# Casting transfers for queries and keys, and three score tiles a batch on VectorE, in a fused attention and soft mixture-of-experts kernel

## The chip, the cores and the metric

One core of a Trainium2 chip. The metric is the device time of one launch in microseconds (us). Every kernel was timed several times beside the kernel before on the same chip. A run can fall in a slower state, here counted from 1.5% above the fastest run of the same kernel.

## The reference, cut to what matters

```python
# q, k, v: 8 batches x 12 heads x 448 x 64, float32; cap = 30
scores = np.matmul(q, k.transpose(0, 1, 3, 2)) / np.sqrt(64)
scores = cap * np.tanh(scores / cap)
attn = softmax(scores)                       # over the keys
x = np.matmul(attn, v)                       # -> 3584 x 768
logits = x @ phi                             # 768 x 32
slot_in = softmax(logits, axis=0).T @ x      # over all 3584 rows
# ... 8 small expert networks on slot_in ...
out = softmax(logits, axis=1) @ slot_out
```

The tanh and the exponential of all scores, 96 heads x 448 x 448 each, are what ScalarE has to do.

## The kernel before: the parts that matter

A *quad* is four heads, a *batch* three quads. The main loop runs 56 iterations j; seven make a batch, and m stands for j mod 7. An iteration has slots a, b, c and d, in which side jobs are issued, so the order of each engine's queue is fixed by the program. The code below is shortened; cuts are marked by dots. Each iteration handles six score tiles of 128x448.

```python
psT = pool("psT", bufs=1, space=PSUM)     # tag "T": one bank for all small transposes and sums
psV = pool("psV", bufs=1, space=PSUM)     # tag "pv": one bank for the value products
...
    def cast(nm, Q):                       # float32 -> bf16 on VectorE, then transposes of 128x128
        t = cst.tile([P, NT, P], BF16, ...)
        dve.tensor_copy(t.rearrange(...), raws.pop((nm, Q)).rearrange(...))
        casts[nm, Q] = t
        if Q > 1:
            load(nm, Q + 1)
...
    shared = [j for j in range(NCH - 2) if j % 7 == 3 and j > 7] if cap < 80 else []
    def poly_exp(j, part):                 # exp of one tile on VectorE, in three parts
        if part == 0:   ...                # three tensor_scalar
        elif part == 1: ...                # two scalar_tensor_tensor
        else:           ...                # two more
...
    def e_norm(b):                         # sum of exp(logits): zps in bank "T", then zacc
        ps = psT.tile([P, 1], F32, name="zps", tag="T")
        ...
            dve.tensor_tensor(zacc, ps, zacc, op=ALU.add)
...
    def spare(n):                          # n filler matmuls into bank "pv"
        busy(n, psV.tile([P, 2, VW], F32, name="junk", tag="pv")[:, 0, 0:P])
...
    for j in range(NCH):                   # one iteration, shortened
        run(j, "0")
        tanh_chunk(2 * j); tanh_chunk(2 * j + 1); exp_chunk(j - 1)   # ScalarE
        pv_pass(pr, 0)                     # TensorE pv; VectorE rec, xq
        run(j, "a")
        qk_chunk(2 * j + 2)                # TensorE scores
        run(j, "b")
        pv_pass(pr, 1)
        run(j, "c")
        qk_chunk(2 * j + 3)
        run(j, "d")
```

The softmax here doesn't subtract the row's maximum and nothing guards it: scores larger than these inputs give would overflow.

## Time and profile before

| | |
|---|---|
| time | 317.54 us median of 3 (317.26 to 317.74) |
| ScalarE | busy 281.3 us, 89% of the span |
| TensorE | busy 269.4 us, 86% |
| VectorE | busy 193.7 us, 62% |
| one batch, from the first scores at m = 4 to the same of the next batch | 32.68 us, five times running |

The chain that ended last is ScalarE for two thirds, and TensorE's waits inside the loop are short. These are the chain by engine ("issue" is time in which an engine waited for nothing that the profile shows), then two rows of the list of waits (who waited for whom: total us, times, longest). In the rows, sc are the scores, kps and qps the transposes of keys and queries, zps and zacc the column sum and its total, pv the value products, rec and xq their scaling, xp, xm and xe tiles of the polynomial, vbd the values that GpSimd casts, and junk the fillers.

```profile
ACT 67%; PE 20%; DVE 5%; issue 3%; DMA 2%; DVEq 0%; ACTq 0%
```

```profile
PE sc L269 <- ACT ex L278: 7.9, 19, 0.7
PE kps L237 <- DVE zacc L383: 1.2, 5, 0.2
```

The scores wait for ScalarE to free their buffer (7.9 us), so TensorE has a little slack. The key transposes wait for zacc for 0.2 us at a time.

### The profile page before, as it was taken

To read this page: it belongs to the slowest core of one execution; us is meant where nothing else is said; L and a number is where in the kernel's file an instruction comes from. 1 tells how busy PE (TensorE), PEld (TensorE's weight loads), DVE (VectorE), ACT (ScalarE), POOL (GpSimd) and SP (SyncE) were. 2 spreads that over 40 slices of the span, in tenths; PEclk is the share of its full clock that TensorE was granted. 3 is DMA by queue.
4 is the path that set the end of the run, shared out by engine and by line. 5 is a ranking of instruction groups with operands and counts; after the bars stand their busy time and mean duration, and the time that the engine had idled before them with its cause. 6 is when DMAs were issued, how large, how long until landed. Compare 5 with 4: busy or idle time off the path is not lost.

```text
span 314.8 us, 8844 instructions
## 1 busy us (share of the span) xinstructions
PE 269.4 (86%) x3804; PEld 191.0 (61%) x3804; DVE 193.7 (62%) x473; ACT 281.3 (89%) x208; POOL 106.5 (34%) x134
## 2 busy tenths in 40 slices
PE   7899898899889998898889989898889998998720
PEld 6667665667666665666666666666666677743400
DVE  3636565766586659575867587657766574327840
ACT  4999999999999999999999999999999999326730
POOL 2464342523543452354245416441732130200000
PEclk9999999999999999999999999999999999999985
DMA  8899999799999999999999999999999807898997
GB/s 223 267 234 238 291 244 269 159 231 256 235 210 231 266 237 207 254 220 266 194 225 269 221 264 190 242 235 266 209 232 254 214 14 207 290 393 301 389 411 314
DMA packets 57479, 77.68 MB, mean 247 GB/s; under 512 B 3809, under 2 KB 53601, under 8 KB 57441
## 3 DMA queue, kind: packets, MB, share of 16 engines
q0 software_dynamic: 30480, 25.22, 52.1%
q1 hardware_dynamic: 26672, 51.68, 48.1%
q8 instruction: 29, 0.48, 0.6%
q10 hardware_dynamic: 288, 0.23, 0.2%
q14 instruction: 10, 0.07, 0.1%
HBM read 91.32 MB, written 18.87 MB: 350 GB/s over the span
## 4 chain that ended last, share of the span: by engine, by line
ACT 67%; PE 20%; DVE 5%; issue 3%; DMA 2%; DVEq 0%; ACTq 0%
ACT ex L278 33%; ACT ex L282 32%; PE pv L318 5%; PE sc L269 3%; PE so_ps L676 2%; PE junk L506 2%; PE hp L649 2%; ACT ob L754 1%; PE op L702 1%; DMA kraw<-in_k_dram 1%; DVE xq L329 1%; PE op L745 1%; PE xps L344 1%; DMA out_dram<-obh 1%; DVE ob L752 1%
## 5 line engine op out<-in xcount | busy, mean ns | idle before, releaser
L278 ACT ACTIVATE ex<-sc 128x1344 bf16<-128x1344 f32 (+1 forms) x113 | 162.3, 1693 | 0.9 <-PE sc L269 0.8
L282 ACT ACTIVATE ex<-ex 128x2688 bf16<-128x2688 bf16 (+4 forms) x58 | 159.2, 2779 | 0.1
L318 PEld LDWEIGHTS <-ex 128*128 128x128 bf16 x1344 | 78.7, 97 | 21.5 <-DVE xq L329 17.8
L318 PE MATMUL pv<-vbd,ex 128*128 128x130 bf16 x1274 | 88.6, 220 | 2.6 <-ACT ex L282 0.7
L269 PE MATMUL sc<-qT,kT 64*64 64x448 bf16 x672 | 78.6, 358 | 8.2 <-ACT ex L278 7.9
L247 POOL CAST vbd<-vraw 64x896 bf16<-64x896 f32 x23 | 21.5, 936 | 103.6 <-PE pv L318 65.3
L269 PEld LDWEIGHTS <-kT 64*64 64x64 bf16 x672 | 27.3, 105 | 25.3 <-issue 7.5
L329 DVE TENSOR_TENSOR xq<-pv,rec 128x256 bf16<-128x256 f32 x91 | 38.6, 424 | 3.1
L328 DVE RECIPROCAL rec<-pv 128x4 f32<-128x4 f32 x91 | 16.5, 181 | 32.1 <-PE pv L318 31.2
L506 PEld LDWEIGHTS <-ones 128*128 128x128 bf16 x470 | 28.6, 100 | 11.6 <-DVE xq L329 8.0
L372 POOL COPY e<-E 128x512 bf16<-128x512 bf16 x9 | 7.2, 795 | 81.5 <-ACT E L366 49.6
L506 PE MATMUL junk<-ones 128*128 128x128 bf16 x433 | 31.4, 219 | 2.5 <-DVE xq L329 1.6
L239 DVE COPY kT<-kps 128x896 bf16<-128x896 bf16 x23 | 14.4, 625 | 24.6 <-PE kps L237 24.4
L109 POOL DMA_DIRECT2D w1b<-in_moe_w_dram x32 | 25.2, 791 | 0.0
L248 POOL CAST vbd<-vraw 64x896 bf16<-64x896 f32 x23 | 23.7, 1029 | 1.3
L346 DVE COPY xT<-xps 128x512 bf16<-128x512 bf16 x47 | 19.5, 415 | 3.2 <-PE xps L344 3.0
L344 PE MATMUL xps<-ident,xq 128*128 128x128 bf16 x188 | 18.1, 218 | 0.2 <-DVE zacc L383 0.2
L239 DVE COPY qT<-qps 128x896 bf16<-128x896 bf16 x23 | 14.2, 616 | 5.2 <-PE qps L237 5.2
L226 DVE CAST kbf<-kraw 128x896 bf16<-128x896 f32 x22 | 16.0, 728 | 1.3 <-DMA kraw<-in_k_dram 1.3
L237 PE MATMUL kps<-ident,kbf 128*128 128x128 bf16 x161 | 12.8, 219 | 4.2 <-DVE slacc L418 2.2
L237 PE MATMUL qps<-ident,qbf 128*128 128x128 bf16 x161 | 12.8, 219 | 3.2 <-DVE lg L360 2.7
L237 PEld LDWEIGHTS <-kbf 128*128 128x128 bf16 x161 | 10.0, 97 | 9.0 <-issue 8.3
(113 smaller groups left out, 255.5 us busy)
## 6 DMA issues: line engine op xcount, KB each, us to landing
w1b<-in_moe_w_dram POOLq DMA_DIRECT2D x32, 384.0 KB, 10.2
vraw<-in_v_dram SPq DMA_DIRECT2D x23, 448.0 KB, 6.6
qraw<-in_q_dram SPq DMA_DIRECT2D x22, 448.0 KB, 7.8
kraw<-in_k_dram SPq DMA_DIRECT2D x22, 448.0 KB, 6.0
w2d<-in_moe_w_dram POOLq DMA_DIRECT2D x20, 384.0 KB, 9.2
w2t<-w2d SPq DMA_DIRECT2D x20, 384.0 KB, 5.9
out_dram<-ob SPq DMA_DIRECT2D x8, 768.0 KB, 7.3
w2b<-in_moe_w_dram POOLq DMA_DIRECT2D x12, 384.0 KB, 9.9
```

Source lines behind the costliest of these rows:

```text
L109: pool.dma_start(out=w1b[e][:, js, fs], in_=w1r[:, e, js, fs])
L237: pe.transpose(ps[:, c, :], src[:, c, :], ident)
L239: dve.tensor_copy(t, ps)
L247: pool.tensor_copy(t[0:HP, :, :, 0:DH], raw[0:HP])
L248: pool.tensor_copy(t[HP:P, :, :, DH + 1:VW - 1], raw[HP:P])
L269: pe.matmul(sc[cs, u, 0:S], qkT["k", Q][r, c, cs], qkT["q", Q][r, :, cs], start=True, stop=True)
L278: act.activation(exs[j][:, half * CS + u0:half * CS + u1, :], sc[:, u0:u1, 0:S], ACT.Tanh, scale=qk_scale / cap)
L282: act.activation(exs[j][:, u0:u1, :], exs[j][:, u0:u1, :], ACT.Exp, scale=cap)
L318: pe.matmul(pvs[pr, half][:, n, 0:VW], exs[j][:, u, GOFF[g]:GOFF[g] + P], vbds[Q % 2][:, h, c, :], start=(c == 0 and n == 0), stop=(c == N ...
L329: dve.tensor_tensor(xq[Q][:, 2 * half:2 * half + 2, h * P:(h + 1) * P] .rearrange("p g (i d) -> p g i d", i=2), pv[:, :, :, 0:DH], rec.to_ ...
L344: pe.transpose(ps[:, g, :], xq[Q][:, g, h * P:(h + 1) * P], ident)
L506: pe.matmul(junk if home is None else home, ones, ones, start=True, stop=True)
```

## The change

Its intent is to relieve ScalarE: two more tiles a batch (m = 1 and m = 6 beside m = 3) get their exponential on VectorE. To make room there, VectorE's casts of queries and keys are dropped for all but the first two quads; the transfers cast on the way, issued by GpSimd. The keys then lie by heads, and fourteen transposes of half width take the place of seven.

```diff
     def load(nm, Q):
-            sp.dma_start(out=t, in_=quad_ap(nm, Q))
+            (sp if nm == "v" else pool).dma_start(out=t, in_=quad_ap(nm, Q))   # bf16 tile for q, k
...
     def transp(nm, Q):
         for c in range(NT):
-            pe.transpose(ps[:, c, :], src[:, c, :], ident)
+            if Q == 1: ...
+            for h in range(2):
+                pe.transpose(ps[h * HP:h * HP + HP, c, :], src[:, h, c * DH:(c + 1) * DH], ident)
...
-    shared = [j for j in range(NCH - 2) if j % 7 == 3 and j > 7] if cap < 80 else []
+    shared = [j for j in range(NCH - 2) if j % 7 in (1, 3, 6) and j > 7] if cap < 80 else []
...
-        at(j + 2, "d" if b == 0 else "a", spare, 4 if b == 0 else 14)
+        at(j + 2, "d" if b == 0 else "a", spare, 4 if b == 0 else 12)
...
     for j in shared:
-        for dj, slot, part in ((0, "a", 0), (0, "c", 1), (0, "d", 2)):
-            at(j + dj, slot, poly_exp, j, part)
+        for slot, part in (("a", 0), ("c", 1)):
+            at(j, slot, poly_exp, j, part)
+        at(*((j, "d") if j % 7 == 3 else (j + 1, "b")), poly_exp, j, 2)
```

Cut: the special path of the first two quads, whose tiles move to a borrowed weight buffer, and the removal of the cast jobs; in their slots the loads are issued now.

## The prediction

> **What bounds the kernel now.** I read the page, then the chain of waits in order of time, then the groups by shape, then one stretch of the timeline. Line numbers are those of the kernel before.
>
> ```profile
> PE 269.4 (86%) x3804; PEld 191.0 (61%) x3804; DVE 193.7 (62%) x473; ACT 281.3 (89%) x208; POOL 106.5 (34%) x134
> ```
>
> The reader is to see that ScalarE and TensorE are both close to full over the span, VectorE far from it.
>
> ```profile
> 56.91 2.36 ACT ex L278 x2
> 59.27 1.96 ACT ex L282
> 61.23 2.36 ACT ex L278 x2
> 63.59 2.33 ACT ex L282
> ```
>
> That is the chain: tanh of two chunks (2.36 us), then exp of one group of six score tiles (2.33 us), without a gap, from about 20 us to 216 us. Where VectorE takes one tile the exp is 1.96 us. So a tile is worth 0.37 us of ScalarE. (The recorded busy time of one tanh grows along the trace while the ends stay 1.18 us apart; I use ends.) A batch is seven loop iterations; I write m for the iteration modulo 7. A batch takes 14 x 1.18 + 6 x 2.33 + 1.96 + 0.20 = 32.7 us.
>
> TensorE is close behind. In most batches it waits for ScalarE to free a score buffer in only three iterations, m = 2, 3, 4:
>
> ```profile
> 183.96 0.75 PE L269 MATMUL sc<-qT,kT 64*64 64x448 bf16 x6 [0.22 <-ACT ex L278]
> ...
> 188.86 0.76 PE L269 MATMUL sc<-qT,kT 64*64 64x448 bf16 x6 [0.52 <-ACT ex L278]
> ...
> 211.95 0.76 PE L269 MATMUL sc<-qT,kT 64*64 64x448 bf16 x6 [0.49 <-ACT ex L278]
> ```
>
> 0.22 + 0.52 + 0.49 = 1.2 us of slack in a batch of 32.7. Its scores finish 1.2 to 2.9 us before ScalarE wants them. The rest of its idle time is waiting for VectorE, one round trip after another, because one PSUM bank serves all small transposes and sums ("T") and one serves the value products ("pv"):
>
> ```profile
> 199.46 0.41 DVE L346 COPY xT<-xps 128x512 bf16<-128x512 bf16 x1
> ...
> 199.79 0.61 DVE L226 CAST kbf<-kraw 128x896 bf16<-128x896 f32 x1
> ...
> 200.72 0.18 DVE L328 RECIPROCAL rec<-pv 128x4 f32<-128x4 f32 x1 [0.31 <-PE pv L318]
> ...
> 200.93 0.42 DVE L329 TENSOR_TENSOR xq<-pv,rec 128x256 bf16<-128x256 f32 x1
> ...
> 201.58 0.16 DVE L383 TENSOR_TENSOR zacc<-zps,zacc 128x1 f32<-128x1 f32 x1 [0.23 <-PE zps L379]
> ...
> 201.79 0.55 PE L237 MATMUL kps<-ident,kbf 128*128 128x128 bf16 x7 [0.25 <-DVE zacc L383]
> ```
>
> Here (m = 6) the key transposes wait until VectorE has read the tiny sum out of their bank. The order of VectorE's queue therefore sets TensorE's pace, however low its share is.
>
> ```profile
> 204.07 0.62 DVE L226 CAST qbf<-qraw 128x896 bf16<-128x896 f32 x1
> ...
> 204.90 0.18 DVE L328 RECIPROCAL rec<-pv 128x4 f32<-128x4 f32 x1 [0.21 <-PE pv L318]
> ...
> 205.46 0.61 DVE L239 COPY qT<-qps 128x896 bf16<-128x896 bf16 x1
> ...
> 206.12 0.35 PE L355 MATMUL lps<-phib,xT 128*128 128x32 bf16 x8
> ```
>
> At m = 0 the logits wait for qT in the same way.
>
> [...] the weight casts are all issued by POOL, 0.78 us each. [...] six score matmuls of 448 columns take 0.57 to 0.76 us, seven full-width transposes of 128 columns 0.56 us. [...] 382 to 394 ns for the polynomial's tensor_scalar steps, 613 to 872 ns for its two-tensor steps on the same 448 elements.
>
> **The change part by part.**
>
> ScalarE: shared groups go from 7 to 20 (m = 1, 3, 6 with j from 8 to 53). 13 x 0.37 = 4.8 us less. A batch falls to 31.9 us. Alone this would give 317.5 - 4.8 = 312.7 us.
>
> VectorE: it loses two casts in each of 22 quads: 22 x (0.728 + 0.660) = 30.5 us. It gains 13 polynomials. One is 0.382 + 0.394 + 0.394 (part 0), 0.613 + 0.626 (part 1), 0.666 + 0.872 (part 2) = 3.95 us; 13 x 3.95 = 51.4 us. Net +20.9 us, 194 to 215 us, still under 70%. As starts in the queue the parts occupy about 1.23, 1.31 and 1.50 us.
>
> TensorE: 44 transposes of seven become fourteen of half width, 308 more matmuls. The two heads write different column halves, so I expect pairs to overlap and the path to grow by only some 0.03 us a call. Two fillers fewer per batch give back about 0.1 us.
>
> GpSimd and the transfers: 44 more issues x 0.78 = 34 us on an engine busy 34% and mostly waiting. The loads are issued a whole quad ahead, with two buffers, and bytes read stay the same; the tightest needs its keys some 2.7 iterations (12 us) after the issue, against a median landing of 10 us for the larger weight pieces. I take these as hidden.
>
> **The path through TensorE and VectorE**, placing the new parts where the emitted order has them, starting from the shown stretch:
> - m = 6: part 0 stands behind xT: 199.87 + 1.23 = 201.1, so rec is 0.4 late, xq ends at 201.7. Part 1 stands before zacc: 201.7 + 1.3 = 203.0, zacc to 203.15, key transposes at 203.2 in place of 201.79: +1.4 us. The cast removed there blocked nothing, since rec was waiting for TensorE.
> - m = 0: shifted by 1.4, xT ends at 205.6. Part 2 follows: 207.1, then rec, in place of 204.90: +2.2. qT and the logits follow: about 208.35 for 206.12, +2.2.
> - m = 1 and 2: part 0 delays the second rec by another 0.5; the fillers wait for it (+2.75). The 0.5 us that TensorE used to wait for ScalarE is used up (+2.15). Then part 2 stands between kT and the logits' addition: 0.65 later, the query transposes wait for their bank: +2.8 at the products of m = 3.
> - m = 3, 4: from the first rec of m = 3 to the products of m = 4 VectorE is continuous already (183.79 to 189.71), unchanged: still +2.8. At m = 4 and 5 nothing is added, and the casts removed there stood beside waits.
>
> So this loop takes about 32.7 + 2.8 = 35.5 us a batch, against ScalarE's 31.9: VectorE's queue and TensorE's waits become the bound, and ScalarE starves by 3.6 us a batch. There are six such passes (j = 13 to 53): 16.8 us, plus about 0.5 for j = 8. TensorE's lead over ScalarE at the end, about 2.5 us, is lost once in return: 317.5 + 17.3 - 2.5 = 332 us. I shade this to 330, as part of VectorE's work may slide into gaps that I took as shut.
>
> **The rivals.**
> - ScalarE stays the bound: 312 to 316 us. For it: the chain is ScalarE for 65% of the span, and VectorE would still be idle over 30%. Against it: only 1.2 us of TensorE slack a batch, of which ScalarE's gain alone takes 0.75.
> - About half of the added VectorE work is hidden: the loop stays near 32 to 33.5 us, 314 to 322 us, within 2%.
> - The half-width transposes do not pair: 7 x 0.056 = 0.39 us a call, six calls a batch, +2.3 us a batch on the loop, total about 345. Against it: the score matmuls pair in this trace.
> - The keys arrive late, behind weight pieces in one queue: several us of TensorE waiting for transfers. Against it: ordering ahead of time; I give it little.
>
> **Range and chances.** The hand-walked loop is my main case, 62%, from 324 to 339. Half-hidden or bound by ScalarE within 2%: 30%. The full 4.8 us is only 1.5%, so faster by over 2% needs a second gain (shorter VectorE queue without the casts); 8%. The range 312 to 339 holds both main cases.
>
> **What would show it.** Right: in the changed profile ScalarE has gaps before tanh released by TensorE's scores, a few us a batch; the key transposes at m = 6 wait over 1 us for zacc; the logits' addition and rec wait behind polynomial steps; batches are about 35 us apart. Wrong: tanh and exp stay back to back with batches of 31.9 us (then VectorE's order did not matter), or TensorE waits for transfers, or seven pairs of transposes take 0.8 us.

## The result, and the profile after

The changed kernel takes 337.63 us (median of 4, 337.00 to 338.95); the kernel before took 317.64 us beside it. The ratio is 1.062 (95% interval 1.056 to 1.068): 6% slower. Ratios here are the mean time of one kernel's fast runs over that of the other's in the same rounds, so not quite the ratio of the medians quoted.

The page of the changed kernel, its engines, its chain and the granted TensorE clock in 40 slices (in tenths):

```profile
PE 279.3 (83%) x4098; PEld 196.8 (58%) x4098; DVE 217.1 (64%) x520; ACT 279.7 (83%) x208; POOL 140.3 (42%) x178
...
PEclk9999999978999799979999999989999999999995
...
PE 42%; DVE 36%; ACT 14%; DMA 3%; issue 2%; DVEq 0%; ACTq 0%
```

The chain has passed from ScalarE to TensorE and VectorE taking turns, though VectorE is busy only 64% of the time. The clock row, which before was 9 everywhere but in the last two slices, has dips. Rows of the list of waits:

```profile
ACT ex L286 <- PE pv L326: 16.2, 9, 3.2
PE kps L245 <- DVE zacc L391: 10.8, 5, 2.2
ACT ex L286 <- PE sc L277: 6.2, 13, 1.2
```

ScalarE now starves for 22 us behind TensorE, and the wait for zacc is 2.2 us where it was 0.2. One such place, m = 6, in the timeline (start, duration, engine, line, operation, out<-in, count, and in brackets the idle time before and what ended it):

```profile
215.59 1.07 POOL L255 CAST vbd<-vraw 64x896 bf16<-64x896 f32 x1 [4.50 <-PE pv L326]
...
216.14 0.25 PE L387 MATMUL zps<-ones,e 128*128 128x1 bf16 x4
216.34 0.80 DVE L308 SCALAR_TENSOR_TENSOR xp<-xm 128x448 f32<-128x448 f32 x1
216.70 1.25 POOL L256 CAST vbd<-vraw 64x896 bf16<-64x896 f32 x1
217.17 1.25 DVE L309 SCALAR_TENSOR_TENSOR xp<-xp,xm 128x448 f32<-128x448 f32 x1
218.35 0.14 DVE L391 TENSOR_TENSOR zacc<-zps,zacc 128x1 f32<-128x1 f32 x1
218.55 0.63 PE L245 MATMUL kps<-ident,kb 128*64 128x128 bf16 x14 [2.16 <-DVE zacc L391]
219.11 1.70 PE L326 MATMUL pv<-vbd,ex 128*128 128x130 bf16 x14
...
222.62 1.29 ACT L286 ACTIVATE ex<-sc 128x1344 bf16<-128x1344 f32 x1 [3.02 <-PE pv L326]
```

Three things are to be seen. The sum of one column, 0.14 us of work, stands behind part 1 of the polynomial. Part 1 itself took 0.80 + 1.25 us, while GpSimd cast v beside it; without a cast beside it the same two operations take 0.61 and 0.62 us (the second 0.91 in three of seven places). The second cast too was longer, 1.25 us where its median in the kernel before is 0.96. And after the wait the pv products took 1.70 us; elsewhere they take 0.98. Windows around two such places, without and with the dip (us, busy and count of PE, PEld, DVE, ACT, POOL, then the granted clock, DMA share, GB/s):

```profile
178.00:182.00 4.00, 2.94 (x39) 1.88 (x37) 3.53 (x10) 4.00 (x3) 1.81 (x2) 1.00 1.30 205
182.00:186.00 4.00, 2.89 (x50) 2.27 (x50) 3.01 (x7) 2.38 (x3) 4.00 (x6) 1.00 0.79 171
...
216.00:220.00 4.00, 1.84 (x31) 1.58 (x28) 3.08 (x5) 3.60 (x3) 3.96 (x5) 0.87 1.18 179
220.00:224.00 4.00, 4.00 (x50) 2.75 (x49) 2.86 (x8) 1.29 (x1) 0.82 (x2) 0.70 1.18 240
```

The clock was granted by half from 218.9 on for 3.41 us. The trace's clock records show this four times in the loop: at 72.2 (for 6.83 us), 109.7, 147.3 and 218.9 (3.41 us each), 17.07 us in all; before there is none before the tail. The records hold two values only, 1.0 and 0.5. The starts lie 37.55, 37.55 and 71.68 us apart, which is 11, 11 and 21 times 3.413, and the stretches are 1 or 2 times 3.413 us long. So the clock changed on a grid of 3.413 us here (an estimate from these starts and lengths). The identical wait at 181 us (2.16 us of TensorE idle, as at 216 us) drew no half clock, and its place in the grid tells the two apart. In the three traces with this wait (changed, f2_v_later, f3_m3_m6) there are 18 of them. With grid lines every 3.413 us from the first start of half clock, the 13 that began 0.0 to 2.2 us after a line were followed by half clock at the next, the 5 that began 2.9 to 3.0 us after one were not. No run moved the grid on purpose. TensorE's busy share of one step of the grid does not decide: in the changed kernel the step from 68.77 us was 64% busy and the clock was lost behind it, that from 181.40 us was 50% busy and the clock was kept. What does decide was not shown.

Where the 22.4 us between the two profiled spans (314.8 and 337.2 us) arose: the six batches from the scores at m = 4 of j = 11 to those of j = 53 took 218.61 us for 196.65, so +21.96; the rest is -0.55 ahead of them and about +1 behind. These are the scores at both ends, first before, then after:

```profile
58.14 0.76 PE L269 MATMUL sc<-qT,kT 64*64 64x448 bf16 x6 [0.52 <-ACT ex L278]
...
254.79 0.76 PE L269 MATMUL sc<-qT,kT 64*64 64x448 bf16 x6
```

```profile
57.59 0.76 PE L277 MATMUL sc<-qT,kT 64*64 64x448 bf16 x6
...
276.20 0.76 PE L277 MATMUL sc<-qT,kT 64*64 64x448 bf16 x6
```

### The profile page after: what moved, and what is told of

Its sections match the earlier page's. It is cut to its first block, busy times and chain, and to the rows that moved or that the text cites. A ratio compares the mean times of both kernels' runs of the same rounds, so it can differ in the third digit from the quotient of the medians.

```text
span 337.2 us, 9443 instructions
## 1 busy us (share of the span) xinstructions
PE 279.3 (83%) x4098; PEld 196.8 (58%) x4098; DVE 217.1 (64%) x520; ACT 279.7 (83%) x208; POOL 140.3 (42%) x178
## 4 chain that ended last, share of the span: by engine, by line
PE 42%; DVE 36%; ACT 14%; DMA 3%; issue 2%; DVEq 0%; ACTq 0%
PE pv L326 15%; DVE xq L337 7%; ACT ex L286 7%; ACT ex L290 6%; PE sc L277 6%; DVE xp L309 4%; PE junk L515 4%; PE kps L245 4%; DVE ex L312 3%; DVE xp L311 3%; DVE rec L336 3%; DVE xm L304 2%; DVE xp L308 2%; DVE xe L306 2%; DVE qT L247 2%
## 5 line engine op out<-in xcount | busy, mean ns | idle before, releaser
L286 ACT ACTIVATE ex<-sc 128x1344 bf16<-128x1344 f32 (+1 forms) x113 | 141.2, 1305 | 22.9 <-PE pv L326 16.2
L290 ACT ACTIVATE ex<-ex 128x2688 bf16<-128x2688 bf16 (+4 forms) x58 | 131.3, 2268 | 0.1
L326 PEld LDWEIGHTS <-ex 128*128 128x128 bf16 x1344 | 81.2, 100 | 28.4 <-DVE xq L337 20.5
L326 PE MATMUL pv<-vbd,ex 128*128 128x130 bf16 x1274 | 92.7, 225 | 5.8 <-DVE xq L337 4.1
L255 POOL CAST vbd<-vraw 64x896 bf16<-64x896 f32 x23 | 23.4, 1017 | 101.5 <-PE pv L326 92.0
L277 PEld LDWEIGHTS <-kT 64*64 64x64 bf16 x672 | 25.7, 106 | 20.0 <-issue 2.3
L245 PE MATMUL kps<-ident,kb 128*64 128x128 bf16 x308 | 13.7, 230 | 15.8 <-DVE zacc L391 10.8
L256 POOL CAST vbd<-vraw 64x896 bf16<-64x896 f32 x23 | 25.7, 1118 | 1.3
L245 PEld LDWEIGHTS <-kb 128*64 128x64 bf16 x308 | 11.6, 114 | 19.1 <-issue 18.8
L309 DVE SCALAR_TENSOR_TENSOR xp<-xp,xm 128x448 f32<-128x448 f32 x20 | 21.6, 1078 | 0.7
L167 POOL DMA_DIRECT2D qb<-in_q_dram x22 | 16.1, 734 | 3.2 <-DVE kT L206 3.2
```

The lines of the kernel that those rows point to most:

```text
L245: pe.transpose(ps[h * HP:h * HP + HP, c, :], src[:, h, c * DH:(c + 1) * DH], ident)
L256: pool.tensor_copy(t[HP:P, :, :, DH + 1:VW - 1], raw[HP:P])
L277: pe.matmul(sc[cs, u, 0:S], qkT["k", Q][r, c, cs], qkT["q", Q][r, :, cs], start=True, stop=True)
L286: act.activation(exs[j][:, half * CS + u0:half * CS + u1, :], sc[:, u0:u1, 0:S], ACT.Tanh, scale=qk_scale / cap)
L290: act.activation(exs[j][:, u0:u1, :], exs[j][:, u0:u1, :], ACT.Exp, scale=cap)
L309: dve.scalar_tensor_tensor(xp, xp, POW2[2], xm, ALU.add, ALU.mult)
```

## The experiments

Twelve kernels ran, all correct. "Six batches" below is the time from the scores at j = 11 to those at j = 53, read from the trace, less the 196.65 us of the kernel before.

### 1. One part alone

The casting transfers and half-width transposes with only the old shared tile:

```diff
-    shared = [... j % 7 in (1, 3, 6) and j > 7]
+    shared = [... j % 7 == 3 and j > 7]
```

> The changed kernel with its transfers and half-width transposes, but only the seven shared tiles of before (m = 3). If VectorE's queue order is the cause, the transfers and transposes are harmless: 315 to 319 us, within 1% of before, chain on ScalarE. If the transposes or late keys cost, 325 us or more, with TensorE waiting for transfers or the transposes taking 0.8 us a call.

Measured: 320.06 us (318.25 to 321.12), just above the range expected; before 317.27, ratio 1.007 (1.003 to 1.011). Five of the six batches take 32.67 us, those of the kernel before to a hundredth, and all six together 0.3 us more, so in the loop this half of the change costs next to nothing and ScalarE is the bound. VectorE is down to 167.2 us. The profiled run had lost 2.8 us by the first full batch (scores at m = 4 of j = 11 at 60.94 us for 58.14), at the start. That points to the run and not to the change: the changed kernel, with the same start, was there at 57.59, and the profiled runs of two other kernels were late too, e2_polys_only (61.28, a slow run), which has the old start, and g1_v_after_sum (60.54), whose four other runs were 2.5 to 4.1 us shorter. Its cause is open.

The kernel before with three shared tiles, placed as in the change:

```diff
-    shared = [... j % 7 == 3 and j > 7]
+    shared = [... j % 7 in (1, 3, 6) and j > 7]
   # and the parts placed as in the change
```

> The kernel before (VectorE casts, plain transfers) with the 20 shared tiles and the places of their parts as in the changed kernel. If VectorE's queue order is the cause: as slow as the changed kernel or a little slower, 336 to 346 us. If the transfers and transposes cause most of the loss: 322 us or less.

Measured: 354.21 us median of four, but three of them, the profiled one too, were slow; the one fast run took 347.11. So no ratio is given, and only the fast run is compared: it is 9.5 us above the changed kernel's median, above the range expected. By this one run, the same loop is worse with VectorE's casts in the queue than with the transfers and half-width transposes in their place, so these did what they were meant to. They were not enough.

### 2. The order at m = 6

The sum zacc issued one slot earlier, ahead of part 1:

```diff
-                at(j + 13, "d", e_norm, b)
+                at(j + 13, "c", e_norm, b)
```

> The changed kernel with the tiny sum and its read (zacc) one slot earlier, ahead of part 1 of the polynomial at m = 6; same work on each engine. If the wait of the key transposes for zacc (2.2 us in a pass) and the half clock that follows it (about 1 us in four of six passes) carry the loss: 15 to 18 us less than the changed kernel, 319 to 323 us. If VectorE's total load is what matters: no change, 335 to 338 us.

Measured: 327.57 us (326.66 to 329.52), ratio 1.033 (1.029 to 1.037). 10 us came back, not 15 to 18. The longest wait for zacc is 0.3 us and no half clock is left in the loop. The rest is not this wait: the batches average 34.4 us, since the tile's other parts still stand in the loop. This edit also moved the sum away from GpSimd's cast and from the half clock, so it can't part the three; experiments 4 and 5 do.

### 3. Which tile costs it

Tiles at m = 1 and 3 only:

```diff
-    shared = [... j % 7 in (1, 3, 6) and j > 7]
+    shared = [... j % 7 in (1, 3) and j > 7]
```

> The changed kernel without the six shared tiles at m = 6 (14 shared tiles). If the loss sits in the m = 6 pass: near ScalarE's bound, 317.5 - 7 x 0.37 = 315 us, up to 319. If it is spread over the added tiles in equal shares: about half of the 20 us remains, 327 us.

Measured: 320.36 us (320.04 to 320.77), just above the range expected; ratio 1.010 (1.008 to 1.011). Batches average 33.3 us, six of them 3.1 us more than before; no half clock in the loop.

Tiles at m = 3 and 6 only:

```diff
-    shared = [... j % 7 in (1, 3, 6) and j > 7]
+    shared = [... j % 7 in (3, 6) and j > 7]
```

> The changed kernel with the shared tiles at m = 3 and m = 6 only (no tile at m = 1). Theory: nearly the whole loss comes from m = 6 (its part 1 before zacc and its part 2 before the next rec), so the time stays within 4 us of the changed kernel's, 333 to 338 us, with batches near 35.3 us. Rival: the loss comes from VectorE's total load, and a tile less gives a third of it back: 328 to 332 us.

Measured: 337.73 us (336.42 to 339.66), ratio 1.062 (1.057 to 1.067), as the changed kernel. With the same number of tiles, m = 6 costs 17 us more than m = 1. So it is the place of the tile and not VectorE's load. The profiled run had 20.5 us of half clock in the loop, the changed kernel's 17.07, and its six batches took 216.44 us for 218.61. By the price found in experiment 5 the difference in half clock is about 1 us, so the m = 1 tile costs the changed kernel some 3 us in six batches (an estimate), which more half clock hides in the totals: the granted clock of this kernel's runs was 0.943 to 0.961, of the changed kernel's 0.961 to 0.972.

### 4. The clock

Filler matmuls that TensorE can do while it waits for zacc:

```diff
                 at(j + 13, "d", e_norm, b)
+                at(j + 13, "d", spare, 32)
```

> The changed kernel with 32 matmuls of 128x128 queued on TensorE behind the sum of zps at m = 6, so that TensorE computes on junk while it waits for zacc. Theory: the 2.2 us wait itself makes the throttle grant TensorE half its clock for 3.4 us behind it, which costs about 1 us in four of the six batches beside the wait; with the filler the granted clock stays near 1.0 behind m = 6 and the time falls by 3 to 6 us, from about 337 to 331 to 334 us, though the wait stays. Rival: the half clock has another cause or costs nothing because ScalarE is the bound there; then the time is the same or up to 2 us more (the filler takes about 1.8 us of a 2.2 us wait) and half-clock stretches stay.

Measured: 333.36 us (333.11 to 333.94), ratio 1.048 (1.044 to 1.052). It is 4.3 us faster than the changed kernel though TensorE has 192 more matmuls to do. The timeline at the same place:

```profile
212.19 0.25 PE L387 MATMUL zps<-ones,e 128*128 128x1 bf16 x4
212.53 1.96 PE L516 MATMUL junk<-ones 128*128 128x128 bf16 x32
214.60 0.58 PE L245 MATMUL kps<-ident,kb 128*64 128x128 bf16 x14
215.12 0.98 PE L326 MATMUL pv<-vbd,ex 128*128 128x130 bf16 x14
```

The transposes come 2.4 us after zps as before (218.55 - 216.14), but the pv products behind them take 0.98 us, not 1.70, and no half clock is recorded in the loop. Six batches: +16.7 us, for +22.0. So 17.07 us of half clock cost 5.3 us.

### 5. The stretch

The first attempt put GpSimd's v cast of m = 6 later in its queue:

```diff
         quad_in(3 * b + 3, (j + 4, "a"), (j + 5, "a"), (j + 4, "d"), (j + 5, "c"),
-                (j + 6, "d"))
+                (j + 7, "d"))
```

> The changed kernel with GpSimd's v cast that falls at m = 6 moved six slots later, to slot d of m = 0 of the next batch, so that it no longer runs beside VectorE's part 1; VectorE's order is as before. Theory: the cast stretches the two part 1 operations from 0.61 and 0.62 to 0.80 and 1.25 us; with it moved the wait for zacc falls from 2.16 to 1.3 to 1.5 us (the prediction's 1.4), the half clock behind it goes too, and the time falls by 6 to 9 us to 329 to 332 us. Rival 1: only the stretch goes and the half clock stays: 332 to 335 us. Rival 2: the wait is set by the order alone and part 1 keeps its length: 336 to 339 us.

Measured: 338.87 us (338.08 to 340.54), ratio 1.066 (1.061 to 1.070); nothing changed, and the experiment failed to do what it was for:

```profile
215.60 1.07 POOL L255 CAST vbd<-vraw 64x896 bf16<-64x896 f32 x1 [2.89 <-PE pv L326]
```

The cast starts at 215.60 as it did at 215.59. GpSimd is idle ahead of it and waits for pv to release the buffer; its queue order doesn't set its start. The second attempt gave the cast something to wait for:

```diff
     def vcast(Q):
+        if Q > 5 and Q % 3 == 0:
+            pool.tensor_copy(vgate, zacc)      # one column; holds the cast until zacc is done
         pool.tensor_copy(t[0:HP, :, :, 0:DH], raw[0:HP])
```

> The changed kernel with GpSimd's v cast at m = 6 held back by a copy of zacc that GpSimd makes first, so that the cast can only start when the sum is done; VectorE's order is as before. (Moving the cast later in GpSimd's queue did not move it: it starts when pv of m = 6 ends, whatever stands before it.) Theory: part 1 at m = 6 shrinks from 0.80 and 1.25 us to 0.61 and 0.62, the wait for zacc from 2.16 to about 1.4 us, which is the prediction's figure, and the half clock behind it goes: 329 to 332 us. Rival 1: the wait shrinks but the half clock stays: 332 to 335 us. Rival 2: the cast held back delays something else (v of the next quad, the loads behind it): 336 us or more, with a new wait in the list.

Measured: 331.21 us (330.00 to 334.07), ratio 1.041 (1.038 to 1.045), in the range of the theory, though some half clock stayed. The timeline at m = 6:

```profile
145.31 0.58 PE L246 MATMUL kps<-ident,kb 128*64 128x128 bf16 x14 [1.35 <-DVE zacc L394]
...
212.88 0.61 DVE L311 SCALAR_TENSOR_TENSOR xp<-xm 128x448 f32<-128x448 f32 x1
...
213.53 0.62 DVE L312 SCALAR_TENSOR_TENSOR xp<-xp,xm 128x448 f32<-128x448 f32 x1
214.07 0.15 DVE L394 TENSOR_TENSOR zacc<-zps,zacc 128x1 f32<-128x1 f32 x1
```

Part 1 takes 0.61 and 0.62 us, and the wait is 1.35 us. Half clock: 6.83 us in the loop (two steps of the grid) in the place of 17.07. Here a wait of 1.35 us of idle TensorE was followed by half clock twice in six batches, and its place in the grid does not tell which: those two began 1.1 and 2.0 us after a grid line, the others 0.4, 0.6, 2.4 and 3.3.

Both cures together, the gate above and this:

```diff
                 at(j + 13, "d", e_norm, b)
+                at(j + 13, "d", spare, 20)
```

> The changed kernel with the v cast of m = 6 held back until zacc is summed (the run at 331.2 us) and 20 matmuls that fill the wait for zacc, so that neither the stretch nor the half clock is left and only VectorE's order is. Theory: the 6.83 us of half clock that were left cost 0.25 us each, as the filler showed (4.2 us for 17.07 us); so 329 to 331 us, which is what the prediction's walk, taken alone, comes to. Rival: with the wait at 1.35 us the filler is itself on the path: 331 to 334 us.

Measured: 329.51 us (329.35 to 329.87), ratio 1.037 (1.032 to 1.042), no half clock in the loop. The four kernels make a square, in us over the six batches of the kernel before:

| | half clock present | filled, none left |
|---|---|---|
| part 1 stretched by the cast | +22.0 (changed kernel, 17.07 us of half clock) | +16.7 |
| part 1 not stretched | +14.0 (6.83 us of half clock) | +11.8 |

Read down the right column, the stretch costs 4.9 us, which is 6 x (2.16 - 1.35) = 4.9. Read across, half clock costs 5.3 us for 17.07 and 2.2 us for 6.83, both 0.31 to 0.32 us for each us of it. Each cell is one trace; by the medians of the whole times the stretch is 3.9 us (333.36 to 329.51) and the half clock 4.3. What is left, 11.8 us, parts further by experiments 1 and 3: 8.7 come with the m = 6 tile even when undisturbed (208.45 us in the kernel with both cures, 199.80 without that tile), 2.8 with the m = 1 tile (199.80, and 196.97 with neither), and 0.3 with the transfers and transposes.

### 6. Attempts to beat both kernels

Tiles at m = 1 and 3, the m = 1 tile's parts moved to where VectorE idles (part 0 in slot c of m = 1, parts 1 and 2 in slot a of m = 2), and 16 fewer fillers a batch:

```diff
-    shared = [... j % 7 in (1, 3, 6) and j > 7]
+    shared = [... j % 7 in (1, 3) and j > 7]
...
     for j in shared:
+        if j % 7 == 1:
+            for dj, slot, part in ((0, "c", 0), (1, "a", 1), (1, "a", 2)):
+                at(j + dj, slot, poly_exp, j, part)
+            continue
   # and the fillers cut as in the next diff
```

> A try to beat both: tiles at m = 1 and m = 3 only, the m = 1 tile's parts put where VectorE idles (part 0 in slot c of m = 1, parts 1 and 2 in slot a of m = 2), and TensorE's filler matmuls at m = 1 and m = 2 cut from 30 to 14. Theory: the loop of TensorE and VectorE, 33.05 us a batch with these two tiles, falls below ScalarE's 32.3 us, and the time is 314 to 317 us, 0 to 1 per cent below the kernel before. Rival: the fillers kept the clock up or lay in waits anyway, and the loop stays at 33: 318 to 321 us.

Measured: 338.89 us (337.99 to 339.07), ratio 1.065 (1.061 to 1.068), with a mean granted clock of 0.917. The same two tiles and fillers, without moving the parts:

```diff
-        at(j + 1, "d", spare, 34 if b == 0 else 10)
+        at(j + 1, "d", spare, 34 if b == 0 else 4)
-        at(j + 2, "d" if b == 0 else "a", spare, 4 if b == 0 else 12)
+        at(j + 2, "d" if b == 0 else "a", spare, 4 if b == 0 else 6)
-            at(j + 2, "c", spare, 8)
+            at(j + 2, "c", spare, 4)
```

> Tiles at m = 1 and m = 3 as in the run at 320.4 us, their parts where the change has them, and only the filler matmuls at m = 1 and m = 2 cut from 30 to 14. It parts the two edits of the run that took 338.9 us. Theory: there it was the moved parts that made TensorE wait 2 us at m = 2 and run at half clock behind it, not the missing fillers; so here no half clock appears in the loop, the batch falls from 33.05 to ScalarE's 32.3 us and the time is 315 to 318 us. Rival: the fillers are what keeps the clock granted; half clock appears at m = 2 to 3 and the time is 325 us or more.

Measured: 325.64 us (324.11 to 327.55), ratio 1.024 (1.019 to 1.028). The rival was right: the fillers keep the clock. Windows of the same stretch of two batches:

```profile
114.00:118.00 4.00, 2.72 (x41) 1.62 (x39) 3.29 (x6) 4.00 (x4) 3.62 (x5) 0.98 0.89 185
118.00:122.00 4.00, 3.79 (x35) 2.51 (x34) 1.88 (x6) 3.44 (x3) 0.42 (x1) 0.50 1.20 194
...
183.00:187.00 4.00, 3.21 (x50) 2.07 (x48) 3.26 (x6) 4.00 (x3) 3.31 (x4) 1.00 1.28 216
187.00:191.00 4.00, 3.25 (x52) 2.42 (x53) 2.94 (x9) 4.00 (x5) 0.00 (x0) 1.00 1.22 234
```

In both batches TensorE's gaps at m = 2 are the same, 0.70 us before the key transposes and 0.80 us before the query transposes; one fell to half clock for 10.24 us and the other did not. Of the four batches without it, two were no shorter than with the fillers (j = 32 to 39 took 33.48 us in both kernels): waits for VectorE took the place of the fillers. The other two were 0.4 and 0.9 us shorter (j = 25 to 32 32.22 for 32.61, j = 46 to 53 33.86 for 34.72), while the whole kernel lost 5.3 us (325.64 for 320.36). Moving the parts on top cost 13 us more, again with half clock, 41 us of it.

Last, the gate of experiment 5 for the cast at m = 1, with two tiles and all fillers:

```diff
-    shared = [... j % 7 in (1, 3, 6) and j > 7]
+    shared = [... j % 7 in (1, 3) and j > 7]
...
     def vcast(Q):
+        if Q > 3 and Q % 3 == 1:
+            pool.tensor_copy(vgate, xp[:, 0:1])    # holds the cast until part 1 is done
```

> A second try to beat both: tiles at m = 1 and m = 3 (the run at 320.4 us), and GpSimd's v cast at m = 1 held back by a one-column copy out of VectorE's part 1, so that the cast no longer stretches part 1 (0.80 and 1.26 us there, against 0.61 and 0.62 without a cast beside it). Behind part 1 VectorE reads the transposed products, for which TensorE's key transposes of m = 2 wait. Theory: the loop of 33.05 us loses 0.8 us and falls just under ScalarE's 32.31; the time is 315 to 317.5 us, 0 to 1 per cent below the kernel before. Rival: the 0.8 us lies beside fillers or other waits; 319 to 321 us as in the run without the gate.

Measured: 320.34 us (319.83 to 322.79), ratio 1.010 (1.005 to 1.014), as without the gate; the rival was right. Part 1 at m = 1 is down to 0.61 and 0.62 us, but TensorE spends the time on fillers:

```profile
179.94 0.83 PE L518 MATMUL junk<-ones 128*128 128x128 bf16 x12
180.20 0.42 DVE L357 COPY xT<-xps 128x512 bf16<-128x512 bf16 x1
...
180.71 0.75 PE L280 MATMUL sc<-qT,kT 64*64 64x448 bf16 x6
```

The scores at 180.71 follow the fillers, which VectorE's earlier copy at 180.20 doesn't move; without the gate they started 2.69 us after the scores ahead of them, and with it as well. No version beat the kernel before.

## Why the prediction was right, and where its terms were off

Mechanism and range were right: 337.6 us in a range of 312 to 339, slower, with ScalarE starving behind TensorE, which waits for VectorE's queue. But 330 is short by 7.6 us, and that is the sum of terms off both ways; that they partly cancelled is luck. To check its steps, here is the mean time over six batches between the starts of neighbouring score chunks (x.1 and x.2 are the first and second chunk whose scores iteration m = x issues), with the last column free of half clock and of the stretch at m = 6:

| step | before | changed | gate and fill |
|---|---|---|---|
| 6.2 to 0.1 (zacc) | 2.77 | 5.50 | 3.93 |
| 0.1 to 1.1 (part 2, qT, logits) | 4.37 | 4.94 | 4.80 |
| 1.1 to 3.1 | 8.96 | 9.16 | 9.16 |
| 3.1 to 4.1 | 4.92 | 4.53 | 4.53 |
| 4.1 to 6.2 | 11.75 | 12.31 | 12.31 |
| sum | 32.78 | 36.44 | 34.74 |

- *m = 6, +1.4.* The wait was right in kind and wrong in size: with the half clock filled (experiment 4) the key transposes came 1.9 us later behind zps than before (2.41 for 0.50), for the walk took part 1 as 1.3 us, from durations without GpSimd's cast beside it. The kernel before could not show the stretch: none of the polynomial's two-tensor operations has a cast beside it there, and part 1 took 0.61 and 0.62 us in all seven places. With the cast held back the wait is 1.35 us (experiment 5) and the step +1.2.
- *m = 0, part 2 ahead of rec and qT, +0.8.* Undisturbed it is +0.4. The walk delayed everything behind part 2 by all of it; where the other half went was not tested.
- *m = 1 and 2, +0.6.* The step is only 0.2 longer than in the kernel before, which waits for ScalarE there. Against kernels without the m = 1 tile, the term was about right: 9.16 us for 8.57 in the kernel with m = 3 and 6 (experiment 3), and 9.16 with m = 1 and 3 for 8.69 with m = 3 alone. TensorE has its fillers there, and with the cast's stretch gone it still did not start sooner (experiment 6).
- *m = 3 and 4, 0.* Taken together 3.1 to 6.2 is 16.84 us for 16.68, so 0.2.
- *Sum.* 35.5 us a batch became 34.74 undisturbed and 36.44 with the two disturbances. The prediction's 16.8 us for six batches is 11.8 undisturbed: 5 us too much. The stretch adds 4.9 and the half clock 5.3, neither of which it had; the 5 us too much hid half of them. The credit of 2.5 us for TensorE's lead was too big as well: ScalarE's last exponential ended 20.5 us later than before and the scores at j = 53 21.4 us later, a credit of 0.9.
- *Half clock.* The prediction did not mention the clock. This is the term that was missing, and the profile before held a hint: filler matmuls in the program that compute nothing.
- *Transposes, +0.03 us a call.* The halves of a pair do start 3 to 31 ns apart at full clock (the paired scores 3 to 4 ns in the kernel before), and from the first start to the last end a call took 0.58 us for 0.55, the +0.03 predicted. But to TensorE's next instruction it took 0.51 us, for 0.40 where value products or fillers follow (four of six calls a batch) and 0.48 where scores follow. That is 0.5 us a batch. With one shared tile it is hidden (experiment 1); no run tested the transposes by themselves in a loop with more tiles.
- *ScalarE, 4.8 us less; transfers hidden.* An exponential of five tiles took 2.08 us for 2.44 of six, so 0.36 a tile for the predicted 0.37, but ScalarE was not the bound and the saving did not show. TensorE waited for no query or key transfer; they landed 6.5 and 8.2 us (median) after the issue.
- *VectorE's load.* The net +20.9 us was +23.4 (217.1 for 193.7).

## What to carry to other kernels

When an engine has work to spare, ask where in its queue the new work stands and who waits behind it: the tile at m = 6 cost 17 us more than the same tile two iterations on, at m = 1, and 10 us came back when a sum of 0.14 us was put ahead of part of its polynomial. Take durations for such a walk from places with the same neighbours, above all for VectorE beside GpSimd (here 0.80 and 1.25 us beside a cast, 0.61 and 0.62 without). And a wait on TensorE can be paid for twice, once as the wait and once in the clock after it: here a gap of 2.16 us was followed by half clock in four of six batches, one of 1.35 us in two of six, and two gaps of 0.70 and 0.80 us, 1.9 us apart, in two of six. Filling the wait with idle matmuls tells the two apart (333.36 us for 337.63 in experiment 4), and a filler already in a kernel should not be taken out before its clock row is read (16 fewer a batch cost 5.3 us in experiment 6).
